# The last matrix product of a fused attention and two-layer kernel, taken as seven products of sums

## The chip, the cores and the metric

The kernel runs as one program on one core of a Trainium2 chip. The metric is the device time of one execution in microseconds (us). Before the change three runs gave 1412.35, 1412.89 and 1417.05 us; the median is 1412.89 us.

TensorE (PE) multiplies: a matmul takes a stationary operand of 128 x 128, loaded by a weight load (PEld) that runs beside the matmul before it, and streams a moving operand past it into PSUM. VectorE (DVE) and ScalarE (ACT) do elementwise work, GpSimd (POOL) works only in the attention, and the queue of SyncE (SP) issues nearly all DMA transfers, in order.

## The reference, cut to what matters

```
x = attention(q, k, v, w_pre, w_post)      # 4 x 448 tokens, 12 heads of 64 -> [1792, 768]
x = sigmoid(x @ w_gate) * (x @ w_val)      # 768 -> 1536
x = x @ w_out                              # 1536 -> 768
h = x @ w_in                               # 768 -> 2048
g = h * sigmoid(1.702 * h)
out = g @ w2_out                           # 2048 -> 768, float32
```

The change is in the last line, and in when its weights are prepared.

## The kernel before, in words

The attention fills about the first 460 us and is not touched. Then come the layers, in two blocks of 896 tokens (t = 0 and 1), in this order: gate, value and `w_out` of block 0; the same of block 1; `w_in` and `w2_out` of block 1; `w_in` and `w2_out` of block 0. Weights arrive as 64-bit floats. A piece of 128 rows by 384 numbers is staged (tile `ws`, five buffers), turned into a 32-bit float by one ACT and four DVE operations (tile `wc`), and, for later blocks, stored in DRAM (`kept`). For precision every operand is a pair: a high part, rounded by ACT, and a low part, which DVE makes by subtracting the high part (`hilo`, and `high`/`low` for weights, tile `w`, five buffers). A product of two pairs is three matmuls: high-high, high-low, low-high.

Several products are already taken by the seven-product scheme of Strassen and Winograd: gate, value and `w_in` (`quarters`, L910) multiply seven sums of quarters of the tokens with seven sums of quarters of the weights (`ORDER` numbers the seven). `w2_out` is not: `second` goes in two halves of its depth. In each half it makes eight feature tiles `hx` (two calls of `inner`) and then, for two column blocks of 384, multiplies eight depth tiles for each of seven token tiles of 128, three matmuls each (L1117). The first half's results are copied to SBUF (`kept`, L1127), the second half's added and written out (L1132 to L1137).

No planner orders this part: it is issued as the Python code runs (`manual_schedule`), each engine's instructions in that order. `take` gives the next weight, `ahead` prepares weights four or five ahead of the one that is multiplied, `after` puts an operation off to the next `flush`, so that DVE does not stand behind ACT.

Of the kernel before, what the change touches and what calls it, by code (L numbers as in the profile page):

```python
# [521 lines left out]
class Ffn:  # L522
# [14 lines left out]
    PW = KG * 128  # L537
    EARLY = 4
# [5 lines left out]
    def __init__(self, ctx, tc, xd, yd, kept, w_gate, w_val, w_out, w2_in, w2_out, out):  # L544
        self.ctx, self.tc, self.nc, self.xd, self.out, self.kept = ctx, tc, tc.nc, xd, out, kept
        self.yd = yd
# [19 lines left out]
        HK = K2 // 2  # L566
        for half in range(2):
            for n in range(self.NN):
                self.pieces += [self.block(w2_out, k0, 1, n * self.PW, self.PW) for k0 in range(half * HK, half * HK + HK)]

# [30 lines left out]
        def second(half, there):  # L601

            for f in range(half * HK, half * HK + HK, 4):
                kept_sums([[o2 + 2 * (f + 2 * g + x) for x in range(2)] for g in range(2)])
            at = range(o3 + half * HK * self.NN, o3 + (half + 1) * HK * self.NN)
            for i in at[::2]:
                if i in there:
                    kept_pair(i)
                else:
                    whole(i)  # L610
                    whole(i + 1)

        o4 = o3 + HK * self.NN
        rest = [*range(o2, o3), *range(o3, o3 + 4), *range(o4, o4 + 4), *range(o4 + 2 * HK - 4, o4 + 2 * HK)]
        early = set(rest)
        for i in range(o2):
            whole(i)
            if i > o1 and i % 2:
                whole(rest.pop(0), False)
        for j in range(0, K1, 2):  # L620
            kept_sums([[4 * (j + f) + 2 * g for f in range(2)] for g in range(2)])
            if j in (4, 8):
                whole(rest.pop(0), False)
        for i in range(o1, o2, 2):
            kept_pair(i)
            for j in range(0 if i in (o1, o2 - 2) else 3):
# [15 lines left out]
        self.turn = 0  # L642

# [4 lines left out]
    def open(self):  # L648
# [4 lines left out]
        self.xy_p = [pool("xy", 2 * self.KD + 1, **rt)] * (2 * self.KD + 1)  # L653
        self.formed = 0
# [6 lines left out]
    def form(self):  # L661

        self.formed += 1
        return self.xy_p[(self.formed - 1) % len(self.xy_p)].tile([128, 2, self.S], F32R, tag="xy", name="xy")
# [138 lines left out]
    def split(self):  # L803
# [6 lines left out]
        while (len(self.staged) < len(self.items) and  # L810
# [10 lines left out]
    def ahead(self):  # L821
        n = self.taken + (4 if self.units[self.used[self.taken - 1]][0] == "f" else 5)
        while self.step < (self.used[n - 1] + 1 if n <= len(self.used) else len(self.units) + 2):
            self.split()
# [55 lines left out]
    def gated(self, g, pg, pv, scale=1.0):  # L880
# [6 lines left out]
        for h in range(2):  # L887
            self.hilo(g[:, :, h], sg[h])
# [6 lines left out]
    def quarters(self, A, done):  # L895
# [26 lines left out]
        for p in self.ORDER:  # L922
            for q in range(2):
# [15 lines left out]
                elif p == 3:  # L939
                    finish(q, 6, x, 1, 0)  # L940
                self.ahead()

    def gates(self, G):
# [3 lines left out]
        def done(q, f, h, y, bank):  # L947
# [3 lines left out]
            else:  # L951
                self.after(0, lambda: self.tt(y, y, sg[f, h], ALU.mult))
                self.after(1, lambda: self.hilo(G[f][:, :, h], y))

        self.quarters(self.A, done)

    def inner(self, HX):

        def done(q, f, h, y, bank):
            self.after(0, lambda: self.nc.scalar.activation(bank, y, AF.Sigmoid, scale=1.702))  # L960
            self.after(1, lambda: self.tt(y, y, bank, ALU.mult))
            self.after(2, lambda: self.hilo(HX[2 * q + f][:, :, h * self.S:(h + 1) * self.S], y))

        self.quarters(self.A, done)
# [72 lines left out]
    def run(self):  # L1037
        nc, ctx, tc, S, KD, K1, K2, NT, PW = (self.nc, self.ctx, self.tc, self.S, self.KD, self.K1, self.K2, self.NT,
                                              self.PW)
        gh_p = ctx.enter_context(tc.tile_pool(name="gh", bufs=K1, **self.kw))  # L1040
        more = 7 * self.KG - len(self.xy_p)
        self.xy_p += [ctx.enter_context(tc.tile_pool(name="xy2", bufs=more, **self.kw))] * more
# [4 lines left out]
        self.pools += [p1] * 4  # L1047
        self.ahead()
        self.xs = {}
        self.ys = {}  # L1050
        self.first(gh_p, 0)
        self.first(gh_p, 1)
        self.second(gh_p, 1)
        self.second(gh_p, 0)

    def first(self, gh_p, t):

        K1, S = self.K1, self.S
        G = []
        for f in range(K1):  # L1060
            G.append(gh_p.tile([128, 2, 2, S], F32R, tag="gh", name="g"))
            if t and f % 2:
                self.gates(G[f - 1:])
# [9 lines left out]
        G = [(g[:, :, 0], g[:, :, 1]) for g in G]  # L1073
        self.next = {p: [] for p in self.ORDER}
        if t:
            self.A = self.next
        steps = K1 // self.KG
        for m in range(self.KD):
            py = self.banks("py", 2)
            for k, _ in enumerate(self.product(py, G)):  # L1080
                if not t and k % self.KG == 0:
                    self.next_a(self.xd[2:], m * steps + k // self.KG,
                                {8 * c + x: [(c, i)] for c in range(self.KG) for i, x in enumerate((0, 4, 6))})
            if t:
                self.next_y(m, py)
            else:
                for h in range(2):
                    y = self.temp("y")
                    self.nc.scalar.copy(y, py[h][:, :S])
                    self.nc.sync.dma_start(self.yd[h][:, m, :], y)  # L1090
        self.A = self.next

    def second(self, gh_p, t):

        nc, S, NT, PW = self.nc, self.S, self.NT, self.PW
        HK = self.K2 // 2
        kept = {}
        for half in range(2):
            HX = []
            for f in range(0, HK, 4):  # L1100
# [100 lines left out]
```

## Time and profile before

| | us |
|---|---|
| median of three runs | 1412.89 |
| the profiled execution | 1417.92 |
| its span, first to last instruction | 1415.9 |
| PE busy in it | 1393.1 (98%) |
| DVE busy in it | 1040.9 (74%) |
| ACT busy in it | 798.5 (56%) |
| `w2_out` matmuls (L1117), 1344 of them, in four stretches of about 58 us | 233.9 |
| `w_in` matmuls (1008 of L910's), four stretches of 51.5 or 51.6 us | 206 |

The profile is of one execution. A line such as "L1117 PE MATMUL po<-w,hx" names the source line, the engine, the operation and the tiles written and read. Busy time counts each moment once, so an engine at 100% has no gap. Durations of neighbouring instructions on DVE overlap a little; what one instruction costs an engine that is full is the distance from its start to the next one's start.

### The profile page before, as it was taken

To read this page: it belongs to the slowest core of one execution; us is meant where nothing else is said; L and a number is where in the kernel's file an instruction comes from. 1 tells how busy PE (TensorE), PEld (TensorE's weight loads), DVE (VectorE), ACT (ScalarE), POOL (GpSimd) and SP (SyncE) were. 2 spreads that over 40 slices of the span, in tenths; PEclk is the share of its full clock that TensorE was granted. 3 is DMA by queue.
4 is the path that set the end of the run, shared out by engine and by line. 5 is a ranking of instruction groups with operands and counts; after the bars stand their busy time and mean duration, and the time that the engine had idled before them with its cause. 6 is when DMAs were issued, how large, how long until landed. Compare 5 with 4: busy or idle time off the path is not lost.

```text
span 1415.9 us, 25571 instructions
## 1 busy us (share of the span) xinstructions
PE 1393.1 (98%) x9120; PEld 1270.5 (90%) x9120; DVE 1040.9 (74%) x2438; ACT 798.5 (56%) x1839; POOL 168.3 (12%) x159
## 2 busy tenths in 40 slices
PE   7999999999999999999999999999999999999998
PEld 5888888888887999999999999899999999999998
DVE  6777677767869675778977878888974887843842
ACT  5877788777979433445445555345733744632631
POOL 2444344334320000000000000000000000000000
PEclk9999999999999999999999999999999999999999
DMA  6644534622436555458952223783252272221222
GB/s 159 186 141 135 158 114 139 178 95 97 159 117 208 165 169 166 147 170 270 293 178 75 62 68 92 258 286 106 79 166 66 71 256 79 72 74 34 68 62 74
DMA packets 188192, 194.37 MB, mean 137 GB/s; under 512 B 66956, under 2 KB 183968, under 8 KB 188064
## 3 DMA queue, kind: packets, MB, share of 16 engines
q1 hardware_dynamic: 187040, 192.49, 43.4%
q8 instruction: 72, 1.18, 0.4%
q14 instruction: 56, 0.46, 0.1%
q10 hardware_dynamic: 960, 0.23, 0.1%
q0 software_dynamic: 64, 0.01, 0.0%
HBM read 113.65 MB, written 40.50 MB: 109 GB/s over the span
## 4 chain that ended last, share of the span: by engine, by line
PE 88%; DVE 5%; ACT 2%; issue 2%; DMA 2%; POOL 1%; SPq 0%; DVEq 0%; POOLq 0%; ACTq 0%
PE pq L910 25%; PE po L1117 16%; PE py L863 11%; PE pso L326 8%; PE pg L863 6%; PE pv L863 6%; PE psv L345 4%; PE psp L281 4%; PE psq L241 4%; DMA gt<-sc 1%; DVE st L288 1%; PE pst L206 1%; ACT ex L295 1%; POOL ghl L274 1%; DVE at L210 1%
## 5 line engine op out<-in xcount | busy, mean ns | idle before, releaser
L910 PE MATMUL pq<-xy,w 128*128 128x448 f32 x1764 | 361.0, 366 | 0.0
L910 PEld LDWEIGHTS pq<-xy,w 128*128 128x128 f32 x1764 | 330.9, 188 | 29.1 <-DVE w L799 0.5
L1117 PE MATMUL po<-w,hx 128*128 128x384 f32 x1344 | 233.9, 336 | 0.2 <-DVE w L799 0.2
L1117 PEld LDWEIGHTS po<-w,hx 128*128 128x128 f32 x1344 | 232.9, 188 | 0.7 <-DVE w L799 0.5
L274 POOL TENSOR_TENSOR ghl<-gt,ghl 120x448 fp32r<-120x448 f32 (+1 forms) x143 | 163.6, 1148 | 240.8 <-ACT ghl L210 182.8
L326 PEld LDWEIGHTS pso<-w,ex 120*112 120x112 f32 (+1 forms) x1440 | 159.0, 177 | 24.5 <-ACT w L308 7.2
L863 PE MATMUL py<-g,w 128*128 128x448 f32 x864 | 175.3, 364 | 0.9 <-DVE g L892 0.9
L326 PE MATMUL pso<-w,ex 120*112 120x120 f32 (+1 forms) x1440 | 172.6, 270 | 3.6 <-ACT w L308 1.9
L863 PEld LDWEIGHTS py<-g,w 128*128 128x128 f32 x864 | 161.9, 187 | 14.0 <-DVE g L892 1.3
L281 PE MATMUL psp<-ghl,wphl 120*120 120x448 f32 x540 | 140.2, 385 | 2.5 <-ACT ex L295 1.7
L288 DVE TENSOR_REDUCE st<-psp 120x1 f32<-120x448 f32 x180 | 108.9, 614 | 33.1 <-PE psp L281 32.4
L799 DVE TENSOR_TENSOR w<-ws,w 128x384 fp32r<-128x384 f32 x152 | 83.4, 554 | 51.4 <-ACT w L793 48.7
L793 ACT CAST w<-ws 128x384 fp32r<-128x384 f32 x152 | 75.4, 508 | 75.9 <-PE po L1117 67.3
L295 ACT ACTIVATE ex<-psp,st 120x448 f32<-120x448 f32 x180 | 113.3, 635 | 8.5 <-DVE st L288 3.6
L732 ACT ACTIVATE wc<-ws 128x384 f32<-128x384 f32 x136 | 75.1, 555 | 58.5 <-DMA ws<-in_moe_w_in_dram 28.5
L281 PEld LDWEIGHTS psp<-ghl,wphl 120*120 120x120 f32 x540 | 88.6, 182 | 17.0 <-ACT ex L295 3.9
L793 ACT CAST w<-wc 128x384 fp32r<-128x384 f32 x92 | 47.2, 513 | 98.9 <-DVE wc L756 96.2
L863 PE MATMUL pg<-xy,w 128*128 128x448 f32 x432 | 91.5, 368 | 0.0
L863 PE MATMUL pv<-xy,w 128*128 128x448 f32 x432 | 91.2, 368 | 0.0
L863 PEld LDWEIGHTS pv<-xy,w 128*128 128x128 f32 x432 | 81.1, 188 | 8.2
L863 PEld LDWEIGHTS pg<-xy,w 128*128 128x128 f32 x432 | 80.9, 188 | 8.2
L210 ACT CAST ghl<-gt 120x448 fp32r<-120x448 f32 (+1 forms) x132 | 74.4, 570 | 16.6 <-PE psp L281 8.4
(92 smaller groups left out, 1853.4 us busy)
## 6 DMA issues: line engine op xcount, KB each, us to landing
gt<-sc SPq DMA_DIRECT2D x172, 210.0 KB
ws<-kept SPq DMA_DIRECT2D x90, 384.0 KB
kept<-wc SPq DMA_DIRECT2D x136, 192.0 KB
ws<-in_moe_w_out_dram SPq DMA_DIRECT2D x56, 384.0 KB
ws<-in_moe_w_in_dram SPq DMA_DIRECT2D x32, 384.0 KB
ws<-in_moe_w_gate_dram SPq DMA_DIRECT2D x24, 384.0 KB
ws<-in_moe_w_val_dram SPq DMA_DIRECT2D x24, 384.0 KB
nat<-in_k_dram SPq DMA_DIRECT2D x48, 112.0 KB
```

Source lines behind the costliest of these rows:

```text
L210: (eng.copy if eng is nc.scalar else eng.tensor_copy)(dst, src)
L274: eng.tensor_tensor(out=t[:m, 1], in0=gt.pop(s)[:m], in1=t[:m, 0].bitcast(F32), op=ALU.subtract)
L281: nc.tensor.matmul(ps[:m, :S], wphl[:m, wp, :m], t[:m, gp], start=(i == 0), stop=(i == 2))
L288: nc.vector.tensor_reduce(out=st[:m, 0:1], in_=pre[s][:m, :S], axis=AX.X, op=ALU.max, negate=True)
L295: nc.scalar.activation(t[:m], pre.pop(s)[:m, :S], AF.Exp, bias=st[:m, 0:1], scale=1.0, accum_out=st[:m, 1:2])
L326: nc.tensor.matmul(ps[:JC, c, :, :n], e[:m, c * JC:(c + 1) * JC], w[:m, :, :n], start=True, stop=True)
L732: self.nc.scalar.activation(c.bitcast(F32), self.staged[self.units[i][1]][:, :, 1].bitcast(F32), AF.Abs)
L793: self.nc.scalar.copy(w[:, 0], self.source(i))
L799: self.nc.vector.tensor_tensor(out=w[:, 1], in0=self.source(i), in1=w[:, 0].bitcast(F32), op=ALU.subtract)
L863: self.nc.tensor.matmul(acc[hb][:, :self.S], st, act[k0 + kc][hb][:, ap], start=(k0 + kc == 0 and part == 0 and ap == 0), stop=(k0 + kc == ...
L910: nc.tensor.matmul(x, st, A[p][c][:, ap], start=(first and c + part + ap == 0), stop=(c == self.KG - 1 and part == 1), skip_group_check=no ...
L1117: nc.tensor.matmul(po[tk][:, :PW], HX[kc][:, part, tk * 128:(tk + 1) * 128], w[:, wp], start=(kc == 0 and part == 0 and wp == 0), stop=(kc ...
```

## The change

`w2_out` over its full depth of 2048 becomes one seven-product scheme: depth halves (8 tiles each) by column halves (384) by token halves (three tiles of 128, `a` and `b`). The seventh token tile (`d`, 128 tokens) is multiplied directly. The seven products run in the order `PHASES`; their results are gathered in six PSUM banks (`U`, `V`, three each), with three ACT copies after each of three products and DVE adds after the next; the direct tile has a bank of its own (`D_bank`).

The sums of the weights, eight pairs of 128 x 384 per depth tile (seven for the products, one for the direct tile), are made once by `sums_out` and stored in DRAM (`sums2`): three depth tiles during gate and value of block 1, two during its `w_out`, three during `w_in` of block 1. `pump` paces this, one call after each weight that is multiplied. `fetch` reads the pairs back, up to nine ahead, into the buffers of `ws` and `w`, five of each in turn; the last ten go to `w`'s five alone. The sums of the activations are made by `form`, up to seven ahead. So `inner` no longer splits its results; it leaves them as plain 32-bit blocks (`raw`). All pieces of `w2_out` are converted earlier: 28 beside gate and value of block 0, the rest in the two `w_out` stages and beside gate and value of block 1. Activation blocks of all kinds now share one list of 45 buffers, taken and given back in order (`form`, `give`).

The core of the diff:

```
-        for there in (early, range(len(self.pieces))):
-            second(0, there)
-            second(1, there)
...
+        rest = [*range(o3, len(self.pieces)), *range(o2, o3)]
         for i in range(o2):
             whole(i)
-            if i > o1 and i % 2:
+            if 6 <= i < o1 and i % 3 or i > o1 and i % 2:
                 whole(rest.pop(0), False)
...
+    def sums_out(self, kcs, ring=3):
+        nc, PW = self.nc, self.PW
+        own = [self.form(F32) for _ in range(3)]
+        x, y, t = (b[:, :, :PW] for b in own)
+        outs = deque(self.form() for _ in range(ring))
...
+        def put(kc, p, src, *after):
+            outs.rotate(1)
+            out = outs[0][:, :, :PW]
+            self.hilo(out, src)
+            self.after(0, lambda: nc.sync.dma_start(self.sums2[kc][p], out.bitcast(F32)))
+            for a in after:
+                self.tt(*a, ALU.subtract)
...
+            self.later_work(self.sums_out(range(3)), 0.62)
...
+            self.later_work(self.sums_out(range(3, 5), 2), 1.4)
...
+    def fetch(self):
+        seq, at = self.loads
+        while self.fetched < len(seq) and self.fetched < self.used_up + 9:
+            j = self.fetched
+            inw = j >= self.TAIL or j // 5 % 2
...
+            w = pool.tile([128, 2, self.PW], F32R, tag=tag, name="wf")
+            self.nc.sync.dma_start(w.bitcast(F32), self.sums2[kc][p])
...
+    TAIL = 54
+    PHASES = (1, 2, 6, 5, 7, 3, 4)
...
+                self.later_work(self.sums_out(range(5, HK)), 0.9)
...
+        for i, (p, kc) in enumerate(order):
+            acc = U if p in (1, 6, 7, 4) else V
+            w = weight()
+            x = H.pop((p, kc))
+            for tk in range(3):
+                matmuls(acc[tk], x[:, :, tk * 128:(tk + 1) * 128], w, kc == 0 and p in (1, 2, 5), kc == HK - 1)
+            self.give(x)
+            if p in (1, 2, 3):
+                matmuls(D_bank, rest_piece(kc + (0 if p == 1 else HK)), w, p == 1 and kc == 0,
+                        p != 1 and kc == HK - 1)
+            elif i in extra:
+                self.fetch()
+                matmuls(D_bank, rest_piece(extra[i]), weight(), extra[i] == 0, False)
...
+            self.flush(False)
+            self.fetch()
+            while forms < len(order) and forms < i + 7:
+                form(*order[forms])
+                forms += 1
...
+            if (p, kc) in soon:
+                self.quarter_a(self.yd, *soon[p, kc])
+            if t and p == 4:
+                self.limit, self.most = self.ends[0][0] + 2 + max(0, kc - 3), self.ends[1][1]
...
+                    while self.step < self.limit:
+                        self.split()
```

On PE, at the end of block 1's `w_out` (py) and behind it, before the change (the last two rows come four times in all):

```order
L863 MATMUL py<-g,w 128x448 x432
L910 MATMUL pq<-xy,w 128x448 x756
L863 MATMUL py<-g,w 128x448 x432
L910 MATMUL pq<-xy,w 128x448 x252
L1117 MATMUL po<-w,hx 128x384 x336
```

The same place now (the last two rows come twice in all):

```order
L875 MATMUL py<-xy,w 128x448 x432
L922 MATMUL pq<-xy,w 128x448 x756
L875 MATMUL py<-xy,w 128x448 x432
L922 MATMUL pq<-xy,w 128x448 x504
L1288 MATMUL po<-wf,xy 128x384 x600
```

The four alternating stretches have become two and two, and 1344 matmuls of `w2_out` are 1200.

On DVE, in the first `inner` call of block 1 before the change (L799 makes a weight's low part, L767 a sum of weights, L919 and L967 work on results, L892 splits one):

```order
L767 TENSOR_TENSOR wt_11966<-ws_11881,wt_11965 128x384
L967 TENSOR_TENSOR s_11906<-s_11906,pq_11865 128x448
L892 TENSOR_TENSOR hx_11758<-c_11908,hx_11758 128x448
L919 TENSOR_TENSOR s_11837<-s_11837,pq_11867 128x448
L799 TENSOR_TENSOR w_11962<-ws_11861,w_11962 128x384
L767 TENSOR_TENSOR wt_11986<-ws_11930,ws_11861 128x384
L767 TENSOR_TENSOR wt_11987<-ws_11930,wt_11986 128x384
L967 TENSOR_TENSOR s_11923<-s_11923,pq_11866 128x448
```

And in the same call now (L811, L779, L931 and L1034 on `s` are the former four; L904 on `xy` makes the low part of a `w2_out` sum, L1034 on `xy_12318<-xy` such a sum):

```order
L779 TENSOR_TENSOR wt_12537<-ws_12441,wt_12536 128x384
L1034 TENSOR_TENSOR xy_12312<-s_12471,pq_12425 128x448
L904 TENSOR_TENSOR xy_12321<-xy_12318,xy_12321 128x384
L1034 TENSOR_TENSOR xy_12318<-xy_12316,xy_12318 128x384
L931 TENSOR_TENSOR s_12400<-s_12400,pq_12427 128x448
L811 TENSOR_TENSOR w_12533<-ws_12423,w_12533 128x384
L779 TENSOR_TENSOR wt_12559<-ws_12498,ws_12423 128x384
L779 TENSOR_TENSOR wt_12560<-ws_12498,wt_12559 128x384
L1034 TENSOR_TENSOR xy_12314<-s_12491,pq_12426 128x448
```

The splits of the results have left this stage, and the sums of `w2_out` for its last three depth tiles stand in it.

On SP, near the end of block 1's first `w2_out` results before the change (`ws<-kept` loads converted weights, `xy<-yd` activations of block 0):

```order
L839 DMA xy_13426<-yd1_130 128x448
L759 DMA kept63_124<-wc_13366 128x384
L726 DMA ws_13464<-kept66_127 128x2x384
L759 DMA kept64_125<-wc_13410 128x384
L726 DMA ws_13530<-kept67_128 128x2x384
L759 DMA kept64_125<-wc_13454 128x384
L726 DMA ws_13568<-kept36_97 128x2x384
```

And in the last of block 1's seven products now (`wf<-sb4_4` is the weight for its depth tile 4, `sb6_4` that for tile 6; `ws<-kept36` and on are block 0's first `w_in` weights):

```order
L1265 DMA out_0_dram<-ot_14323 128x384
L1187 DMA wf_14332<-sb4_4_167 128x768
L851 DMA xy_14336<-yd0_129 128x448
L851 DMA xy_14337<-yd0_129 128x448
L851 DMA xy_14341<-yd1_130 128x448
L851 DMA xy_14340<-yd1_130 128x448
L1187 DMA wf_14357<-sb5_4_175 128x768
L738 DMA ws_14361<-kept36_97 128x2x384
L738 DMA ws_14363<-kept38_99 128x2x384
L738 DMA ws_14365<-kept37_98 128x2x384
L738 DMA ws_14367<-kept39_100 128x2x384
L738 DMA ws_14369<-kept40_101 128x2x384
```

The load of `sb6_4` comes directly behind these: four activation loads and five `w_in` loads now stand between the last loads of `w2_out`'s weights, which PE waits for.

## Rows read from the trace of the kernel before

**Rows 1.** Page, busy time, share of the span, instructions.

```profile
PE 1393.1 (98%) x9120; PEld 1270.5 (90%) x9120; DVE 1040.9 (74%) x2438; ACT 798.5 (56%) x1839; POOL 168.3 (12%) x159
```

**Rows 2.** Page, chain that ended last, by engine and by line.

```profile
PE 88%; DVE 5%; ACT 2%; issue 2%; DMA 2%; POOL 1%; SPq 0%; DVEq 0%; POOLq 0%; ACTq 0%
PE pq L910 25%; PE po L1117 16%; PE py L863 11%; PE pso L326 8%; PE pg L863 6%; PE pv L863 6%; PE psv L345 4%; PE psp L281 4%; PE psq L241 4%; DMA gt<-sc 1%; DVE st L288 1%; PE pst L206 1%; ACT ex L295 1%; POOL ghl L274 1%; DVE at L210 1%
```

**Rows 3.** Waits of PE, longest first: us in total, times, longest.

```profile
PE psp L281 <- ACT ex L295: 1.7, 2, 1.4
PE py L863 <- DVE g L892: 0.9, 1, 0.9
...
PE po L1117 <- DVE w L799: 0.2, 1, 0.2
```

**Rows 4.** PE in order of time: start us, us, instruction, count.

```profile
1242.52 58.41 PE L1117 MATMUL po<-w,hx 128*128 128x384 f32 x336
1300.76 51.62 PE L910 MATMUL pq<-xy,w 128*128 128x448 f32 x252
1352.22 58.40 PE L1117 MATMUL po<-w,hx 128*128 128x384 f32 x336
```

**Rows 5.** Stretches: us, then busy us by engine, granted clock, DMA share, GB/s.

```profile
460.00:641.00 181.00, 181.00 (x955) 164.64 (x952) 121.35 (x293) 71.89 (x145) 0.00 (x0) 1.00 0.54 166
641.00:728.30 87.30, 87.30 (x433) 80.94 (x432) 80.40 (x191) 41.78 (x87) 0.00 (x0) 1.00 0.84 277
728.30:883.00 154.70, 154.70 (x758) 141.76 (x757) 116.91 (x229) 82.02 (x173) 0.00 (x0) 1.00 0.24 73
971.50:1022.80 51.30, 51.30 (x254) 47.31 (x253) 44.59 (x87) 35.62 (x74) 0.00 (x0) 1.00 0.22 62
993.50:1008.20 14.70, 14.70 (x74) 13.54 (x73) 14.63 (x30) 9.92 (x21) 0.00 (x0) 1.00 0.15 45
1147.00:1158.00 11.00, 11.00 (x65) 11.00 (x64) 10.05 (x21) 5.30 (x11) 0.00 (x0) 1.00 1.04 389
```

**Rows 6.** DVE in order of time, while it is full.

```profile
662.77 0.62 DVE L892 TENSOR_TENSOR xy<-xs,xy 128x448 fp32r<-128x448 f32 x1
663.30 0.62 DVE L849 TENSOR_TENSOR xy<-xy 128x448 fp32r<-128x448 f32 x1
...
665.31 0.55 DVE L799 TENSOR_TENSOR w<-wc,w 128x384 fp32r<-128x384 f32 x1
665.78 0.35 DVE L738 TENSOR_SCALAR wc<-wc 128x384 f32<-128x384 f32 x1
666.05 0.55 DVE L750 SCALAR_TENSOR_TENSOR wc<-ws,wc 128x384 uint32<-128x384 uint32 x1
```

**Rows 7.** Page, a costly ACT group: busy us, mean ns.

```profile
L210 ACT CAST ghl<-gt 120x448 fp32r<-120x448 f32 (+1 forms) x132 | 74.4, 570 | 16.6 <-PE psp L281 8.4
```

**Rows 8.** DMA issues: count, KB each.

```profile
ws<-kept SPq DMA_DIRECT2D x90, 384.0 KB
...
out_dram<-ot SPq DMA_DIRECT2D x28, 192.0 KB
...
xy<-yd SPq DMA_DIRECT2D x12, 224.0 KB
```

**Rows 9.** The end, in order of time.

```profile
1404.74 5.88 PE L1117 MATMUL po<-w,hx 128*128 128x384 f32 x33
...
1411.13 1.49 DVE L967 TENSOR_TENSOR ot<-ot,kept 128x384 f32<-128x384 f32 x3
1411.71 1.33 SPq L1134 DMA_DIRECT2D out_dram<-ot  x3
```

**Rows 10.** PE near the start, the same shape twice.

```profile
8.25 1.47 PE L241 MATMUL psq<-kq 64*120 64x448 f32 x6
...
15.51 0.87 PE L241 MATMUL psq<-kq 64*120 64x448 f32 x6 [0.19 <-DVE kq L210]
```

**Rows 11.** The first stretch, columns as in rows 5.

```profile
0.00:10.00 10.00, 4.34 (x20) 3.20 (x21) 2.94 (x8) 2.58 (x4) 4.38 (x16) 1.00 0.65 140
```

More of the change, by code (lines that the diff above doesn't have):

```diff
@@ L1 @@
 import itertools
+from collections import deque
 from contextlib import ExitStack
@@ L537 @@
     PW = KG * 128
+    MORE = 32
     EARLY = 4
@@ L565, in __init__ @@
         o3 = len(self.pieces)
[L566 to L569, printed above, removed]
+        HK = self.HK = K2 // 2
+        self.o3 = o3
+        self.pieces += [self.block(w2_out, half * HK + kc, 1, n * self.PW, self.PW)
+                        for kc in range(HK) for n in range(self.NN) for half in range(2)]
         self.items = []
@@ L625, in __init__ @@
             kept_pair(i)
-            for j in range(0 if i in (o1, o2 - 2) else 3):
+            for _ in range(2 if i % 4 else 1):
                 if rest:
@@ L629, in __init__ @@
         assert not rest
-        for there in (early, range(len(self.pieces))):
-            second(0, there)
-            second(1, there)
+        self.ends = []
+        for t in range(2):
+            for f in range(0, K2, 4):
+                kept_sums([[o2 + 2 * (f + 2 * g + x) for x in range(2)] for g in range(2)])
+            self.ends.append((len(self.units) + 2, len(self.items)))
+            self.units += [("x", None, None)] * 3
+        self.limit, self.most = self.ends[0]
         self.want = set(self.used)
@@ L940, in quarters, with gates @@
                     finish(q, 6, x, 1, 0)
+                if last and q:
+                    self.give(*A[p])
                 self.ahead()
-    def gates(self, G):
+                self.pump()
+    def gates(self, G, last):
         sg = {}
@@ L1050, in run, with first @@
         self.ys = {}
[L1051 to L1056, printed above, removed]
+        self.first(0)
+        self.first(1)
+        self.second(1)
+        self.second(0)
+    def first(self, t):
         K1, S = self.K1, self.S
         G = []
+        if t:
+            self.later_work(self.sums_out(range(3)), 0.62)
         for f in range(K1):
-            G.append(gh_p.tile([128, 2, 2, S], F32R, tag="gh", name="g"))
+            G.append([self.form() for _ in range(2)])
             if t and f % 2:
-                self.gates(G[f - 1:])
+                self.gates(G[f - 1:], f == K1 - 1)
+                if f == K1 - 5:
+                    self.rush()
             elif not t:
@@ L1163 @@
     yd = [dram.tile([128, H // 2, S], F32, name=f"yd{b}") for b in range(2)]
+    sums2 = [[dram.tile([128, 2, Ffn.PW], F32, name=f"sb{i}_{p}") for p in range(8)]
+             for i in range(moe2_w_out.shape[0] // 256)]
     pad = ctx.enter_context(tc.tile_pool(name="pad", bufs=1, side="right"))
@@ L1167 @@
         weights = [w.bitcast(U32) for w in (moe_w_gate, moe_w_val, moe_w_out, moe2_w_in, moe2_w_out)]
-        second = Ffn(ctx, tc, xd, yd, kept, *weights, out)
+        second = Ffn(ctx, tc, xd, yd, kept, sums2, *weights, out)
         attention(tc, q, k, v, w_pre, w_post, xd, second)
```

293 lines of the change are left out of this document (211 added, 82 removed).

## The prediction, made before the change was run

> **What bounds the kernel now.** I read the page's busy times first: PE is busy for 1393.1 of 1415.9 us, DVE for 74% and ACT for 56% of the span [rows 1]. The chain of waits agrees: 88% of it runs over PE, and 16% of the span over the matmuls of `w2_out`, line L1117 [rows 2]. The waits of PE say how firmly: behind the attention there are two, 0.9 us in block 1's `w_out` and 0.2 us in L1117 [rows 3]. So in the layers only fewer matmuls, or cheaper ones, can save time, and the other engines' work is free until it makes PE wait.
>
> PE's timeline gives the unit prices. The 336 matmuls of one quarter of `w2_out` run from 1242.52 to 1300.76, so 0.1733 us each; the 14 weights of one `w_in` call take the 51.46 us to 1352.22, so 3.68 us each [rows 4].
>
> **What the change removes.** 1344 matmuls of the same shape become 1200: per block 7 products x 8 depth tiles x 3 token tiles x 3 matmuls are 504, and the direct tile 16 x 2 x 3 = 96. So 144 go, at 0.1733 us: -25.0 us. With them goes the 0.2 us wait of L1117. The matmuls that stay load one stationary operand each, as before, so I leave their price alone.
>
> The end gets shorter too. Before, the last matmul ends at 1404.74 + 5.88 = 1410.6, three adds on DVE at 1412.6, and the last store lands 3.3 us later, at the end of the span [rows 9]: 5.3 us. Now a result of the last product is only copied (about 0.5 us, since no add follows) and stored: 0.5 + 3.3 = 3.8, so -1.5 us. Bounds: 0, if the three stores queue as before, and -2.0.
>
> **What it adds to DVE and ACT.** A full DVE issues a 448-wide operation every 0.53 us, a 384-wide one every 0.47 and a 384-wide TENSOR_SCALAR every 0.27 [rows 6]. I counted the instructions that the order of the change puts beside each stage's matmuls:
> - Gate and value of block 0 (most of the 181 us from 460 on): 28 more pieces are converted. DVE has 154 x 0.27 + 202 x 0.47 + 53 x 0.53 = 165 us. Before it had 121 in this stage; the next one, block 0's `w_out`, had 80.4 of 87.3 us, 92%, and PE waited nowhere in it [rows 5, 3]. The same share now lasts for longer. I take 0.
> - Gate and value of block 1 (the 154.7 us from 728 on): 12, 173 and 89 of the three kinds, 132 us [rows 5]. Block 1's `w_out`, as long as block 0's: 36, 84 and 31, 66 us, less than before.
> - `w_in` of block 1 (28 x 3.68 = 103 us): the splits of the results leave, but the sums for three depth tiles come in: 132 x 0.47 + 70 x 0.53, and 4 narrow ones that I put at 0.2, make 100 us, 97%. ACT has 151 instructions, at 0.57 us at most [rows 7] 86 us.
> - The product stages (104 us each) have 67 and 46 us on DVE.
>
> Only the 97% is close. Two facts cover it. Weights are prepared at least four ahead, so DVE may be 4 x 3.68 = 14.7 us late before PE notices; adding up its work weight by weight along the order, it falls at most 4 us behind. And DVE can be full without hurting: from 993.5 to 1008.2 it was busy for 14.63 of 14.70 us and PE for all of it [rows 5]. I take 0; the upper bound is the third case below. `rush` issues five sums at once in the middle of block 1's gates, on three buffers, so ACT waits there for a store; two such waits of 3.3 us and the 4 us stay under 14.7.
>
> **What it adds to the queue.** `sums2` is 64 pairs of 393 kB (384 KB in [rows 8]), written once and read twice. A product stage reads 25.2 MB in 104 us, 242 GB/s, and in products 5 and 7, where every second depth tile needs a weight for the direct tile as well, 24 pairs and four activation loads in the 29.1 us of 168 matmuls: 10.4 MB, 356 GB/s. The trace shows the engines moving 389 GB/s for 11 us when they are full [rows 5]. So there is just enough, and nine loads ahead are 11 us of cover at the fastest use (1.21 us each).
>
> One place has no such cover: the last product of block 1. Its last loads use five buffers only, so the load of depth tile 6 is issued late, behind what SP has sent since the product before ended: four stores of 197 kB, four activation loads of 229 kB, the weights for tiles 4 and 5 and five `w_in` loads of 393 kB [rows 8], and then itself. That is 0.79 + 0.92 + 8 x 0.393 = 4.85 MB, at 389 GB/s 12.5 us. The first store is issued some 0.6 us after the product before ends; a lone store needs 3.3 us, 0.5 of them to move, so 2.8 us of latency come on top. The load lands at 0.6 + 2.8 + 12.5 = 15.9 us. PE wants it after six weights of nine matmuls, 6 x 1.56 = 9.4 us. It waits 6.5 us, partly already for tiles 4 and 5. Block 0 has no activation and `w_in` loads there, so no wait. Bounds: 0, if the engines serve the late load beside the earlier ones, and about 10 with the clock case below.
>
> The Trainium skill (DMA: Bandwidth & Descriptors, section Queues, rings and completion order) says that each DMA engine consumes the descriptors of one queue in ring order. By that rule the late load waits for the nine DMAs ahead of it and the 6.5 us stand; without it they would be 0. No row of this trace shows a load overtaking another.
>
> **The sum.** Against the profiled span: 1415.9 - 25.0 - 0.2 - 1.5 + 6.5 = 1395.7 us. The profiled execution took 1417.92 us, 2.0 beside its span and 5.0 above the median of the runs; I take the difference, -20.2, off the median: 1412.9 - 20.2 = **1392.7 us**.
>
> **The rivals.**
> 1. *The queue does not hold up the last product*: 1412.9 - 26.7 = 1386.2 us. For it: the service order of the DMA engines is not seen in the rows. Against it: 4.85 MB must pass in 9.4 us, 516 GB/s, and the best row has 389.
> 2. *The wait costs more than itself.* After the first wait for a DMA, six matmuls took 1.47 us, and the same six took 0.87 us 7 us later [rows 10]. If PE starts again in that way, some 7.6 us at 1.69 times the price lose 3.1 us: 1395.8 us. The granted clock reads 1.00, the upper of its levels, in that stretch [rows 11], so the row doesn't show that it is the clock.
> The Trainium skill (TensorE: Matmul & The Clock Gate, section Why this matters for your kernels) warns that a gap between bursts of matmuls sends the clock back to the lower level; by that rule this rival follows from the forecast's own wait. The trace has slow matmuls after its only long wait, with a granted clock that doesn't tell.
> 3. *DVE becomes the bound in block 1's `w_in`.* In the nearest row DVE was busy for only 44.6 of 51.3 us, 87% [rows 5]. If the rest was not slack but waiting in line (behind ACT's high parts, and ACT behind the stores of the sums), 100 us of work need 115, +12.2: 1404.9 us. If gate and value of block 0 suffer alike (165 / 0.87 = 190, +9), 1414 us, which is no change. Against it: the 14.63 of 14.70.
> 4. *The loads starve PE, and the kernel is slower.* Each product now needs a fresh pair from DRAM within 1.2 to 2.1 us. The gain is gone when the two product stages stretch by 20.2 us together, to 114 us each: 25.2 MB / 114 us = 221 GB/s is the point from which it decides. If the engines gave only the 166 GB/s that they moved in gate and value [rows 5], each stage would take 152 us: 1392.7 + 96 = 1489 us. For it: every load waits in SP's single queue for a release by PE, and each new store stands ahead of it. Against it: 166 GB/s was at a share of 0.54, and 389 GB/s was reached.
> That the change doesn't do what it says is excluded on PE: the order shows 1200 matmuls of the same shape.
>
> **How the numbers follow.** A difference under 0.3% (4.2 us) can't be told from none here. The forecast has 0.47, rival 1 0.25, rival 2 0.13, rival 3 0.06 for the smaller and 0.03 for the larger price, rival 4 0.06. Faster by over 0.3%: 0.47 + 0.25 + 0.13 + 0.06 = 0.91; within it 0.03; slower 0.06. The range of 8 in 10 runs from rival 1's 1386 to 1402, which takes in rival 2, 10 us of wait, and half of rival 3's smaller price.
>
> **What would show it.** Right: about 1200 matmuls at 0.173 us in two stretches, the first some 6 us longer than 104; PE waiting there for a DMA into `wf`, in the last product alone; DVE near 97% in block 1's `w_in` with PE unbroken; 4 us or so between the last matmul and the end. Wrong: waits of PE for DVE in `w_in` of block 1 or in block 0's gate and value, waits for `wf` in products 5 and 7, matmuls over 0.18 us in the mean, or two product stretches of equal length.

## The result, and the profile after

The change made the kernel slower: the changed kernel took 1435.25 us in the median of four runs (1430.63 to 1438.10) beside 1413.72 us for the kernel before (four runs on the same chip), a ratio of 1.0146 with a 95% interval of 1.0112 to 1.0179. The forecast was 1392.7 us. The profiled execution took 1434.26 us, its span is 1432.3.

The page of the profile after, with the rows that answer to [rows 1, 2]: busy time, share of the span and instructions; the chain that ended last, by engine; and four of its costliest groups.

```profile
PE 1379.0 (96%) x8976; PEld 1253.3 (88%) x8976; DVE 1097.6 (77%) x2590; ACT 820.1 (57%) x1921; POOL 168.4 (12%) x159
...
PE 75%; DVE 11%; DMA 6%; ACT 4%; issue 2%; SPq 1%; POOL 0%; DVEq 0%; ACTq 0%; POOLq 0%
...
L922 PE MATMUL pq<-xy,w 128*128 128x448 f32 x1764 | 368.3, 370 | 18.1 <-DVE w L811 18.0
...
L1288 PE MATMUL po<-wf,xy 128*128 128x384 f32 x1200 | 212.1, 339 | 6.1 <-DMA wf<-sb 6.1
...
L904 DVE TENSOR_TENSOR xy<-xy 128x384 fp32r<-128x384 f32 (+1 forms) x208 | 101.3, 510 | 70.0 <-ACT xy L903 69.7
L903 ACT CAST xy<-xy 128x384 fp32r<-128x384 f32 (+1 forms) x208 | 93.1, 477 | 92.6 <-DMA sb<-xy 47.3
```

The 144 matmuls are gone, but PE's share of the chain fell from 88% to 75%: DVE and DMA now stand in it. The last row is the one to stop at. L903 makes the high parts, those of the sums among them, and ScalarE stood idle before it for 47.3 us until a store `sb<-xy`, that is, the store of an earlier sum, had landed.

The waits of PE after, in total, times and longest, where [rows 3] had 0.9 and 0.2 us behind the attention:

```profile
PE pq L922 <- DVE w L811: 18.0, 10, 6.3
PE py L875 <- ACT w L805: 7.8, 3, 3.4
PE po L1288 <- DMA wf<-sb: 6.1, 2, 4.4
...
PE py L875 <- DVE w L811: 1.3, 2, 0.6
```

Only the third was forecast, at 6.5 us. The other 27 us are for weights (`w`) that DVE or ACT had not finished. PE's order of time puts each stage's length beside the forecast (us, from the stage's first matmul to the next stage's first; "block 1" is done ahead of block 0 in the last two layers):

| stage | before | forecast | after | last version (below) |
|---|---|---|---|---|
| attention | 458.3 | 458.3 | 455.9 | 456.6 |
| gate and value, block 0 | 182.6 | 182.6 | 179.2 | 179.2 |
| `w_out`, block 0 | 87.4 | 87.4 | 87.4 | 87.4 |
| gate and value, block 1 ("the gates") | 154.7 | 154.7 | 171.8 | 162.3 |
| `w_out`, block 1 | 88.6 | 88.6 | 99.5 | 87.4 |
| `w_in`, block 1 | 102.6 | 102.6 | 114.8 | 104.2 |
| products, block 1 | 116.9 | 110.5 | 113.4 | 107.9 |
| `w_in`, block 0 | 102.9 | 102.9 | 102.1 | 105.1 |
| products, block 0 | 116.6 | 104.0 | 104.6 | 104.7 |
| behind the last matmul | 5.3 | 3.8 | 3.8 | 4.0 |

The sums of the columns are the spans within 0.3 us. Of the 36.6 us between the forecast's span (1395.7) and the measured one, +17.1, +10.9 and +12.2 lie in the three stages in which sums are made, +2.9 in block 1's products; the first two rows give 5.9 back. The two product stages together came down by 15.5 us; 19.0 were forecast. The same stages as stretches (us, busy us by engine with instructions, granted clock, DMA share, GB/s), `w_out` of block 0 ahead of them, which answers to the second of [rows 5]:

```profile
635.10:722.50 87.40, 87.40 (x434) 81.00 (x433) 79.47 (x189) 42.36 (x89) 0.00 (x0) 1.00 0.87 286
722.50:894.20 171.70, 158.92 (x757) 144.02 (x755) 137.83 (x279) 91.12 (x195) 0.00 (x0) 0.97 0.44 144
894.20:993.70 99.50, 92.89 (x432) 83.78 (x432) 68.56 (x150) 38.23 (x85) 0.00 (x0) 0.95 0.70 234
993.70:1108.40 114.70, 106.92 (x504) 95.11 (x505) 101.81 (x207) 69.29 (x152) 0.00 (x0) 0.99 0.51 169
1108.40:1221.90 113.50, 107.38 (x603) 106.78 (x602) 69.36 (x144) 41.67 (x96) 0.00 (x0) 0.97 0.77 262
```

The busy times are what the forecast had counted: 137.8 us of DVE in the gates (132 forecast), 68.6 in `w_out` (66), 101.8 in `w_in` (100), 69.4 in the products (67). So the work was not mis-sized by more than 6 us. In `w_out` no engine but PE is near full (DVE 69%, ACT 38%), DVE has less to do than before (68.6 us in place of 76.8), and yet the stage takes 10.9 us more; what is missing is not capacity. Four waits of PE make 6.5 us. Nearly as much lies in the matmuls: the 432 took 92.9 us, where block 0's took 87.4, at a mean granted clock of 0.95; it reads 0.50 behind the waits of 1.83 and 3.42 us. ScalarE and SyncE in that stage, in order of time (start, us, instruction, and in brackets the idle time before it and what ended it):

```profile
927.38 0.52 ACT L903 CAST xy<-xy 128x384 fp32r<-128x384 f32 x1 [1.31 <-DMA sb<-xy]
936.55 0.51 ACT L903 CAST xy<-xy 128x384 fp32r<-128x384 f32 x1 [8.65 <-DMA sb<-xy]
...
939.52 0.50 ACT L805 CAST w<-ws 128x384 fp32r<-128x384 f32 x1
```

```profile
929.85 0.42 SPq L735 DMA_DIRECT2D ws<-in_moe_w_in_dram  x1
930.36 9.95 SPq L1016 DMA_DIRECT2D sb<-xy  x3
```

ScalarE has a sum to copy into one of the two output blocks of this stage's ring and stands 8.65 us until the store out of that block has landed; the weight's copy (L805) is behind it in program order. DVE stands too (7.9 us, until 937.97), and PE's wait of 1.8 us at 940.07 follows. The store it waited for could be sent only when DVE had the low part at 929.6; SyncE issued it at 930.36, behind three loads and two stores of weights, and it landed 6 us later.

The gates have another place. ScalarE in the burst, columns as before:

```profile
827.66 0.51 ACT L805 CAST w<-ws 128x384 fp32r<-128x384 f32 x1
...
833.60 0.51 ACT L903 CAST xy<-xy 128x384 fp32r<-128x384 f32 x1 [1.25 <-DMA sb<-xy]
835.04 0.51 ACT L903 CAST xy<-xy 128x384 fp32r<-128x384 f32 x1 [0.93 <-DMA sb<-xy]
836.55 0.51 ACT L903 CAST xy<-xy 128x384 fp32r<-128x384 f32 x1 [1.00 <-DMA sb<-xy]
...
837.39 0.51 ACT L805 CAST w<-wt 128x384 fp32r<-128x384 f32 x1
```

For 9.7 us no weight is copied, since `rush` has put the sums left over in front of them; PE's wait of 6.28 us ends at 838.18. Behind it the granted clock is 0.50, the lower of TensorE's levels (1.2 GHz), for about 4 us:

```profile
832.00:838.20 6.20, 0.02 (x1) 0.03 (x1) 3.91 (x9) 3.01 (x7) 0.00 (x0) 0.78 0.84 303
838.20:840.00 1.80, 1.80 (x5) 1.64 (x6) 1.39 (x3) 1.80 (x5) 0.00 (x0) 0.50 0.72 261
840.00:842.00 2.00, 2.00 (x7) 1.80 (x6) 0.81 (x2) 0.14 (x1) 0.00 (x0) 0.50 0.00 0
842.00:844.00 2.00, 2.00 (x10) 1.82 (x10) 2.00 (x5) 0.40 (x1) 0.00 (x0) 0.94 0.00 0
```

The 99 matmuls from there took 22.35 us, 0.226 each, in place of 154.7 / 756 = 0.205: 2.1 us on top of the wait. The waits in the gates (6.28, 1.19, 2.77 and the 2.56 that ends at 894.23) make 12.8 of the 17.1 us lost there. The lower clock makes most of the rest: behind the wait of 2.77 us it reads 0.50 once more, and the next 115 matmuls took 25.09 us, 1.6 over the same price.

### The profile page after: what moved, and what is told of

Read it like the earlier page. It is cut to its first block, busy times and chain, and to the rows that moved or that the text cites. A ratio compares the mean times of both kernels' runs of the same rounds, so it can differ in the third digit from the quotient of the medians.

```text
span 1432.3 us, 26034 instructions
## 1 busy us (share of the span) xinstructions
PE 1379.0 (96%) x8976; PEld 1253.3 (88%) x8976; DVE 1097.6 (77%) x2590; ACT 820.1 (57%) x1921; POOL 168.4 (12%) x159
## 4 chain that ended last, share of the span: by engine, by line
PE 75%; DVE 11%; DMA 6%; ACT 4%; issue 2%; SPq 1%; POOL 0%; DVEq 0%; ACTq 0%; POOLq 0%
PE pq L922 20%; PE po L1288 15%; PE pso L327 8%; PE pg L875 6%; PE pv L875 6%; PE py L875 6%; PE psv L346 5%; PE psp L282 5%; PE psq L242 4%; DMA sb<-xy 2%; DVE xy L904 1%; DVE w L811 1%; DMA gt<-sc 1%; ACT ex L296 1%; DVE xy L1034 1%
## 5 line engine op out<-in xcount | busy, mean ns | idle before, releaser
L922 PE MATMUL pq<-xy,w 128*128 128x448 f32 x1764 | 368.3, 370 | 18.1 <-DVE w L811 18.0
L1288 PE MATMUL po<-wf,xy 128*128 128x384 f32 x1200 | 212.1, 339 | 6.1 <-DMA wf<-sb 6.1
L1288 PEld LDWEIGHTS po<-wf,xy 128*128 128x128 f32 x1200 | 211.2, 190 | 6.8 <-issue 6.7
L875 PE MATMUL py<-xy,w 128*128 128x448 f32 x864 | 180.4, 370 | 9.1 <-ACT w L805 7.8
L875 PEld LDWEIGHTS py<-xy,w 128*128 128x128 f32 x864 | 164.8, 191 | 24.6 <-ACT w L805 8.9
L904 DVE TENSOR_TENSOR xy<-xy 128x384 fp32r<-128x384 f32 (+1 forms) x208 | 101.3, 510 | 70.0 <-ACT xy L903 69.7
L903 ACT CAST xy<-xy 128x384 fp32r<-128x384 f32 (+1 forms) x208 | 93.1, 477 | 92.6 <-DMA sb<-xy 47.3
L296 ACT ACTIVATE ex<-psp,st 120x448 f32<-120x448 f32 x180 | 113.1, 634 | 9.6 <-DVE st L289 3.6
L805 ACT CAST w<-wc 128x384 fp32r<-128x384 f32 x72 | 36.9, 513 | 73.6 <-DVE wc L768 67.8
```

Source lines behind the costliest of these rows:

```text
L296: nc.scalar.activation(t[:m], pre.pop(s)[:m, :S], AF.Exp, bias=st[:m, 0:1], scale=1.0, accum_out=st[:m, 1:2])
L875: self.nc.tensor.matmul(acc[hb][:, :self.S], st, act[k0 + kc][hb][:, ap], start=(k0 + kc == 0 and part == 0 and ap == 0), stop=(k0 + kc == ...
L903: self.nc.scalar.copy(dst[:, 0], src)
L904: self.after(n, lambda: self.nc.vector.tensor_tensor(out=dst[:, 1], in0=src, in1=dst[:, 0].bitcast(F32), op=ALU.subtract))
L922: nc.tensor.matmul(x, st, A[p][c][:, ap], start=(first and c + part + ap == 0), stop=(c == self.KG - 1 and part == 1), skip_group_check=no ...
L1288: nc.tensor.matmul(acc[:, :PW], x[:, part], w[:, wp], start=(start and part == 0 and wp == 0), stop=(stop and part == 1), skip_group_check ...
```

## The experiments

My theories were, by place: A, ScalarE stands in line for the stores of the sums, because their rings are short; A2, the burst in the gates; B, the sums' work itself fills DVE; C, the six whole pieces that the gates convert in two bunches; and for the products, the forecast's queue. The first eight kernels ran once each. Single executions of one kernel lie up to 7.5 us apart, so these are judged by their stages, which repeat: with nothing changed there, `w_out` of block 1 took 99.5, 100.1, 101.4 and 99.9 us in four kernels, its `w_in` 114.8, 114.7, 114.7 and 114.7.

| kernel | time | gates | `w_out` 1 | `w_in` 1 | products 1 | `w_in` 0 |
|---|---|---|---|---|---|---|
| after | 1434.3 | 171.8 | 99.5 | 114.8 | 113.4 | 102.1 |
| longer rings | 1415.3 | 168.6 | 89.0 | 109.1 | 113.5 | 102.4 |
| even pace | 1426.7 | 164.6 | 100.1 | 114.7 | 113.1 | 102.1 |
| loads in order, third step | 1434.9 | 171.8 | 101.4 | 114.7 | 106.3 | 106.1 |
| sums on GpSimd | 1428.4 | 175.8 | 87.6 | 110.9 | 114.5 | 102.1 |
| rings, pieces spread | 1418.9 | 166.3 | 87.4 | 109.1 | 114.7 | 102.4 |
| rings, split 3/3/2 | 1432.4 | 167.9 | 104.4 | 105.6 | 113.0 | 102.2 |
| loads in order, second step | 1432.8 | 171.3 | 99.9 | 114.7 | 112.2 | 102.1 |
| all, split 3/3/2 | 1421.4 | 162.5 | 102.6 | 106.9 | 112.8 | 102.8 |
| all, split 3/2/3 | 1405.7 | 162.5 | 87.4 | 109.1 | 108.8 | 103.6 |
| all, two pairs of inputs | 1402.7 | 162.3 | 87.4 | 104.2 | 107.9 | 105.1 |

(The time of the last two is a median of five; the stages are those of the profiled execution.)

**Longer rings.**

```
-            self.later_work(self.sums_out(range(3)), 0.62)
+            self.later_work(self.sums_out(range(3), 5), 0.62)
...
-            self.later_work(self.sums_out(range(3, 5), 2), 1.4)
+            self.later_work(self.sums_out(range(3, 5), 7), 1.4)
...
-                if m == self.KD - 1:
+                if m == self.KD - 2:
                     self.rush()
...
-                self.later_work(self.sums_out(range(5, HK)), 0.9)
+                self.later_work(self.sums_out(range(5, HK), 5), 0.9)
```

> Rings of 5, 7 and 5 output blocks for the sums (3, 2 and 3 in the changed kernel), on blocks that lie free there; the rings are given back one row of w_out earlier. Theory A (ScalarE stands in line for the store of an earlier sum): its waits for the stores of the sums fall from 47.3 us to under 10, w_out of block 1 goes from 99.5 to 89 to 91 us, w_in of block 1 from 114.7 to about 110, the gates from 171.8 to about 168 (their burst stays); 1434 becomes about 1417. Theory B (the sums' own work on VectorE and ScalarE is too much, wherever the stores land): the waits for the stores go, but the three stretches keep their lengths within 2 us and the time stays at 1431 to 1436.

The same arithmetic, DMAs and order of issue but for the give-back, and 19 us less: -3.2, -10.5 and -5.6 us in the three stages. ScalarE's waits for these stores:

```profile
ACT xy L903 <- DMA sb<-xy: 7.2, 2, 5.4
```

47.3 became 7.2 us; of the 47.3, 39.6 had lain in `w_out`, 4.5 in `w_in` and 3.2 in the gates. Theory A is shown, for all of the loss in `w_out` and about half of that in `w_in`. The gates kept their burst, with a wait of 3.7 in place of 6.3 us.

**Even pace in the gates**, on the changed kernel's short rings.

```
-            self.later_work(self.sums_out(range(3)), 0.62)
+            self.later_work(self.sums_out(range(3)), 0.75)
```

> The sums of the gates at 0.75 items a step in place of 0.62, so that none are left for the burst after the eighth row. Theory A2 (the burst puts five sums in front of the weights' copies): TensorE's wait of 6.3 us and the 2 us at the lower clock behind it go, the gates take 162 to 165 us in place of 171.8; 1434 becomes about 1426. Theory B (the work itself is too much there): the 6.3 us come back as smaller waits on VectorE's w, the stretch stays at 169 to 173 and the time at 1431 to 1436.

A2 holds: the gates took 164.6 us, of the 6.28 us wait 1.0 is left, in three waits, and the clock stays at 1.00 behind them. The later waits of the gates (1.19, 2.63 and 1.89 us here) stay.

**Order of the loads at the end of block 1's products**, in two variants: `kc >= 2` and, below, `kc >= 1`.

```
-            if t and p == 4:
+            if t and p == 4 and kc >= 2:
```

> At the end of block 1's products the loads of block 0's w_in are staged from the third step of the last product on, not from its first, so the last two loads of the sums stand ahead of them. Theory of the prediction (these loads wait in the queue behind five others): the two waits of 6.1 us on the loads of the sums and about 2 us at the lower clock go, the stretch takes 105 us in place of 113.4; w_in of block 0 may start 1 to 2 us later; 1434 becomes 1427 to 1429. Rival (the load is late by the transfers' rate, not by its place): a wait of 4 to 6 us stays.

The products took 106.3 us, 7.1 less, and one wait of 1.4 us was left: the forecast's reason for the late load holds. But `w_in` of block 0 took 4.1 us more, since its own loads now start later; of the gain 3.0 us stay. The time itself doesn't show it (the attention and `w_out` of block 1, not touched, took 3.6 us more in this execution).

**The sums on GpSimd.**

```
-            self.hilo(out, src)
-            self.after(0, lambda: nc.sync.dma_start(self.sums2[kc][p], out.bitcast(F32)))
+            nc.gpsimd.tensor_copy(out[:, 0], src)
+            nc.gpsimd.tensor_tensor(out=out[:, 1], in0=src, in1=out[:, 0].bitcast(F32), op=ALU.subtract)
+            nc.gpsimd.dma_start(self.sums2[kc][p], out.bitcast(F32))
             for a in after:
-                self.tt(*a, ALU.subtract)
+                nc.gpsimd.tensor_tensor(out=a[0], in0=a[1], in1=a[2], op=ALU.subtract)
```

> The arithmetic of the sums and their stores' issue on GpSimd, which has nothing to do in these layers, in place of ScalarE, VectorE and SyncE; buffers, pace and loads unchanged. Theories A and B alike (the sums stand in line with the weights' copies): the gates about 158, w_out of block 1 about 89, w_in of block 1 about 104; waits of TensorE on VectorE's w under 3 us in all; about 1434 - 14 - 10 - 10 = 1400. Theory C (six more whole pieces in the gates starve the five load buffers): 4 to 5 us of waits stay between 860 and 894 and the gates take 162 to 164. Rival (GpSimd slows VectorE or is itself late): VectorE's operations get longer, the stretches keep their lengths.

The rival held where DVE is busy: `w_out` fell to 87.6, but the gates rose to 175.8, and `w_in` only came down to 110.9, where 104 were expected. The gates' stretch here, and DVE's splits of the weights in `w_in` of block 1 (mean ns behind the bar):

```profile
726.80:902.60 175.80, 158.97 (x758) 140.17 (x756) 152.82 (x243) 80.68 (x171) 75.55 (x84) 1.00 0.44 141
```

```profile
L811 DVE TENSOR_TENSOR w<-wt,w 128x384 fp32r<-128x384 f32 x32 | 27.6, 863 | 0.0
...
L931 DVE TENSOR_TENSOR s<-s,pq 128x448 f32<-128x448 f32 x23 | 14.1, 611 | 0.4 <-PE pq L922 0.3
```

With 36 instructions fewer than in the changed kernel DVE was busy for 15 us more in the gates. The split took 863 ns in place of 548 (changed kernel, same stage); L931, which reads one of its inputs from PSUM, kept its 611.

**The six pieces spread**, on the longer rings.

```
-            for _ in range(3 if j >= K1 - 4 else 0):
+            for _ in range(1):
```

> The rings of 5, 7 and 5 blocks (this kernel took 1415.3), and the six whole pieces that the gates convert for later stand one after each pair of rows, no longer three after each of the last two. Theory C (the bunched pieces hold the five load buffers, so the pieces of w_out come late): the waits at 859, 863 and 891 us (1.2, 2.7 and 2.1) and the clock behind them go, the burst's 3.7 stays; the gates take 161 to 163 us in place of 168.6; 1415 becomes 1407 to 1409. Rival (those waits are VectorE's or ScalarE's fullness there): they come back in other places, the gates stay at 167 to 170 and the time at 1413 to 1417.

In between: the three waits named went, but six of 0.4 to 0.95 us came ahead of the burst. Gates and `w_out` together took 253.7 in place of 257.6 us. So theory C was right about the place, but part of the gain was lost to new waits; that these come from DVE's fullness is not shown. The time shows nothing, since gate and value of block 0 took 182.6 here (see the end).

**Another split**, three depth tiles of the sums in `w_out` and two in `w_in`, on the longer rings.

```
-            self.later_work(self.sums_out(range(3, 5), 7), 1.4)
+            self.later_work(self.sums_out(range(3, 6), 7), 2.1)
...
-                self.later_work(self.sums_out(range(5, HK), 5), 0.9)
+                self.later_work(self.sums_out(range(6, HK), 5), 0.65)
```

> The rings of 5, 7 and 5 blocks, and three depth tiles of the sums in w_out of block 1 (two before) and two in its w_in (three before). Theory B2 (VectorE, at 98 of 109 us, is nearly full in w_in of block 1, and its unevenness makes weights late): w_in goes from 109.2 to 104 to 105 us, since VectorE has some 6 us less there, and w_out stays under 91 (VectorE 79 of 89); 1415 becomes 1410 to 1412. Rival (w_out becomes full in its turn, by VectorE or by the transfers at 280 GB/s plus 3.5 MB): w_out goes to 93 to 97 and the time stays at 1413 to 1418.

Both at once. `w_in` fell to 105.6: with one depth tile less DVE has 95.8 us there and PE hardly waits, so the sums' own work there makes the second half of the loss in `w_in`. This edit takes work off DVE and ScalarE alike; that DVE is the one that is full (theory B2) is borne out by the sums on GpSimd, where ScalarE had only 58.4 us in `w_in`, DVE 107.7 of 111.0, and the stage still took 110.9. `w_out` rose to 104.4 with DVE at 71%, and ScalarE's waits there name a cause that I had not had:

```profile
ACT xy L903 <- DMA xy<-kept: 23.4, 3, 8.8
```

This time it stands for the loads of the sums' own inputs: they are issued two empty items ahead, and at 2.1 items a step that is one step.

**The order again, from the second step**, on the changed kernel.

> As the changed kernel, but the loads of block 0's w_in are staged from the second step of the last product of block 1 on: behind the load for its seventh depth tile, ahead of that for its eighth. From the third step on, the products took 106.3 in place of 113.4, but w_in of block 0 106.1 in place of 102.1. Theory (each load's place in the queue decides): the wait of 4.4 us goes and the one of 1.8 stays, products 107 to 109, w_in 103 to 104; these two stretches together 210.5 to 212.5 (215.5 in the changed kernel, 212.5 from the third step). Rival (the eighth tile's load then comes late instead): products 111 to 113.

The rival held: the eighth tile's load came late instead, with a wait of 3.8 us, and the products took 112.2.

**All together, with the split 3/3/2.**

> All together: rings of 5, 7 and 5, 0.75 items a step in the gates, the six pieces spread, three depth tiles of the sums in w_out and two in w_in, the loads of block 0's w_in from the second step on. If the causes are separate, their gains add: 1415.3 less 4 (pace), 7 (pieces), 4 (split), 4 (order): about 1396 to 1400, with the gates at 157 to 159, w_out 89 to 91, w_in 104, products 108, w_in of block 0 103. If VectorE's fullness is behind them all, the stretches take 5 to 10 us more than that, and the time is 1403 to 1410.

Neither sum came out: 1421.4. The gates lost 6 us and took 162.5, where the sum had 157 to 159; the products kept the late load and took 112.8, where it had 108; and `w_out` kept the waits for its inputs (21.9 us of ScalarE's time) and took 102.6, where it had 89 to 91. So the gains did not add up.

**All together, with the split of the changed kernel, and with two pairs of inputs.** The second one's edit in `sums_out`, beside the split 3/3/2 and rings of 5:

```
-        own = [self.form(F32) for _ in range(3)]
+        own = [self.form(F32) for _ in range(5 if two else 3)]
...
                 yield lambda kc=kc, p=p, src=src, after=after: put(kc, p, src, *after)
+                if two and p == 6 and kc != kcs[-1]:
+                    yield lambda kc=kc: load(kc + 1)
```

> What helped, put together with the split of the changed kernel (three depth tiles of the sums in the gates, two in w_out, three in w_in): rings of 5, 7 and 5, 0.75 items a step in the gates, the six pieces spread, the loads of block 0's w_in from the third step of the last product on. Theory (lateness of in-order queues, each with its own place): gates 162 to 163, w_out 87.4 to 89, w_in 109 (VectorE is full there), products 106, w_in of block 0 103 to 106, in all 1403 to 1408, 0.6 to 0.9 per cent faster than the kernel before. Rival (what is gained in one place is given back by the next, as in the kernel with all edits and the other split, 1421): 1412 to 1418, no difference from the kernel before.

> As the kernel beside it, but three depth tiles of the sums in w_out and two in w_in, where w_out took 102 to 104 us: ScalarE stood 23.4 us, in three waits, in line for the loads of the sums' own inputs, issued too few items ahead at the higher rate. Now these inputs have two pairs of buffers in w_out, the next pair loaded six items ahead, with a ring of 5. Theory D (the loads' lead is what cost there): w_out 88 to 91, w_in 105 to 106, 1400 to 1405. Rival (VectorE or the transfers, 280 GB/s plus one more depth tile's 3.9 MB, do not carry a third): w_out stays at 96 to 104, the time at 1412 to 1420.

Measured: 1405.73 us (1404.12 to 1407.07) and 1402.74 us (1400.67 to 1403.30), beside 1414.60 us for the kernel before, nine runs: ratios of 0.9938 (0.9925 to 0.9950) and 0.9917 (0.9904 to 0.9931). Both beat both kernels, as the theory had it; of the first one's stages only the products missed its range (106 expected, 108.8 measured). The slowest of the second's five runs lies 9.0 us under the fastest of the nine, more than the 3.4 us by which one stage differs between executions (see the end). The stages of the second, gates to products:

```profile
723.20:885.40 162.20, 157.02 (x757) 140.94 (x756) 138.24 (x281) 91.53 (x197) 0.00 (x0) 1.00 0.48 153
885.40:972.80 87.40, 87.40 (x433) 81.01 (x433) 76.73 (x167) 41.93 (x92) 0.00 (x0) 1.00 0.95 325
972.80:1077.10 104.30, 103.13 (x506) 94.56 (x506) 92.42 (x186) 64.74 (x141) 0.00 (x0) 1.00 0.42 135
1077.10:1185.00 107.90, 105.20 (x602) 104.61 (x601) 63.80 (x133) 39.38 (x92) 0.00 (x0) 1.00 0.82 272
```

`w_out` carries a third depth tile's sums at a DMA share of 0.95, with PE busy throughout. ScalarE's waits in it:

```profile
ACT xy L903 <- DMA sb<-xy: 15.6, 7, 4.3
...
ACT xy L903 <- DMA xy<-kept: 3.1, 1, 3.1
```

The waits for the inputs fell from 23.4 (split 3/3/2) to 3.1 us; theory D holds. The first row says something else: 15.6 us of waits for stores are back, on a ring of five, the longest 4.3 us, and PE does not notice. It is not the sum of such waits that costs, but how long one stands beside the weights that are ready. The granted clock is 1.00 in every one of these stretches; behind the waits that are left it doesn't fall. DVE has 138.2 us in the gates, as in the changed kernel, and the stage takes 9.5 us less.

## Why the prediction was wrong, step by step

- *What goes* was right. The 1200 matmuls took 104.6 / 600 = 0.174 us each in block 0's products, and 3.8 us lie behind the last of them: in the end that answers to [rows 9] only one copy, on ScalarE, follows the last matmul (at 1428.56), and the last of three stores follows it.

```profile
1425.80 2.76 PE L1288 MATMUL po<-wf,xy 128*128 128x384 f32 x15
```

```profile
1428.60 0.48 ACT L1283 COPY ot<-po 128x384 f32<-128x384 f32 x1 [0.56 <-PE po L1288]
```

- *The late load of the last product* was right in place, cause and size (6.1 for 6.5 us), and it came with its clock: 113.4 us in place of 110.5. That was rival 2, which I had as an alternative with 0.13; but the lower clock belongs to the forecast's own wait and is no alternative to it, and in the layers of this kernel 0.50 is granted behind the waits of 6.28, 2.77, 3.42, 3.33 and 4.38 us alike. (By the forecast's own list fifteen transfers stand ahead of the late load, not nine; its sum has them all.) By the Trainium skill's rule on gaps between bursts (TensorE: Matmul & The Clock Gate, section Why this matters for your kernels), cited there, the clock had to fall; here the trace agrees, 0.50 behind the waits of 6.28 and 4.38 us.
- *The step that failed* is "What it adds to DVE and ACT ... I take 0", above all "two such waits of 3.3 us and the 4 us stay under 14.7". I summed durations engine by engine and set the sum against four weights of cover. The sums were right within 6 us and the conclusion wrong, for two reasons. The first is the cover. The row of 51.46 us holds two calls of `inner`, not one, and DVE makes 28 low parts in it, not 14:

```profile
L799 DVE TENSOR_TENSOR w<-wt,w 128x384 fp32r<-128x384 f32 x16 | 8.9, 556 | 0.0
L799 DVE TENSOR_TENSOR w<-ws,w 128x384 fp32r<-128x384 f32 x12 | 6.6, 553 | 1.8 <-ACT w L793 1.8
```

So a weight of these stages serves nine matmuls and lasts 1.84 us, and four of them last 7.4 us, not 14.7. The two waits of 3.3 us and the 4 us of the forecast are more than that. Nor was the cover full: pairing each low part with its weight's first matmul, in the kernel before DVE was done in the median only 2.4 us ahead of PE in the gates and about 2 in block 1's `w_in`. In `w_out` a weight serves 18 matmuls, so that four last 14.6 us; there only the second reason is left: each of these engines works in program order. A sum's copy that has no free block stops ScalarE, the weights' copies behind it, then DVE, whose low parts wait for the high ones, and the stores behind DVE's low parts in SyncE's queue: a circle that no busy time shows. I saw it for the burst (three blocks) and not for `w_out`, where the ring has two blocks and [rows 5] had the DMA engines at a share of 0.84 in block 0's stage. It was worth 10.5 us there, 5.6 in `w_in` and 3.2 in the gates.
- In the burst the cover failed as well: ScalarE made no weight for 9.7 us, of which only 3.2 were waits for stores. I had counted waits and not the work ahead of the weights, the five sums' on both engines. DVE had finished the last weight ahead of it at 829.7, and PE ran out at 831.9. Even pacing gave back 7.2 us.
- *"Only the 97% is close. Two facts cover it"* also failed, on its own: with long rings `w_in` still took 109.1 us, and 105.6 with one depth tile less. The row with 14.63 of 14.70 us showed that a full DVE can go unharmed for 15 us, not for 100.
- *Rival 3* named the mechanism, "waiting in line (behind ACT's high parts, and ACT behind the stores of the sums)", and its +12.2 us for `w_in` were measured as +12.2. The match in size is luck: the rings made only 5.6 of them, and the rest stayed without those waits. I gave it 0.09 in all and let it act in one stage, where the order put the same ring into three. Its "gate and value of block 0" was the wrong second place; that stage makes no sums and lost nothing.
- *Rival 4*, my only chance of a slower kernel (0.06), didn't happen: outside the last product no wait for `wf` was long enough to show.

What stays open: 7.6 us in the gates of the last version (5.2 of them in waits of 0.3 to 1.4 us, with DVE at 85%), and whether sums put off into block 1's products, where DVE has room (64 of 108 us), would bring them back. That wasn't tried.

## What to carry to other kernels

Before costing added work at nothing beside a fuller engine, follow one item of it through the queues: what it must find free (a block of a ring, a landed load), who is behind it in program order, and how long that can stand. Read the cover from a trace, as the time between the end of a weight's preparation and its first use, and not from the number of buffers. A ring must cover a store's landing time at the rate of issue, and a load's lead shrinks when the rate rises; neither shows in busy times. Where a stage without a full engine loses time, look first for the row in which an in-order engine waits for a DMA.

## What the runs showed of the hardware

DVE beside GpSimd: a subtraction of two SBUF operands took 863 ns in place of 548, one with a PSUM operand 611 as before. The Trainium skill (SBUF — State Buffer, section SBUF: two separate sides) says that DVE with two SBUF inputs and a reading GpSimd lock each other out of a port pair; the trace agrees.

Gate and value of block 0 has two paces: 864 matmuls in 179.2 us in eight kernels, in 182.6 in the other four, the kernel before among them. It seems to go by the execution and not by the code, since the longer rings and the spread pieces have the same instructions there; no kernel was profiled at both paces. 50 us of each:

```profile
500.00:550.00 50.00, 50.00 (x249) 46.34 (x248) 46.62 (x117) 24.31 (x49) 0.00 (x0) 1.00 0.84 269
```

```profile
500.00:550.00 50.00, 50.00 (x243) 45.41 (x243) 47.26 (x119) 24.65 (x50) 0.00 (x0) 1.00 0.82 266
```

PE is busy throughout in both, at a granted clock of 1.00, and does 249 or 243 matmuls. The cause is open; single runs can differ by these 3.4 us.
